# A mixture-of-experts kernel on one core: the routing's intermediate values in a PSUM bank of their own

## The chip, the core and the metric

The kernel runs on one core of one Trainium2 chip. Its engines are TensorE (PE in the profile; PEld is its loading of weights), VectorE (DVE), ScalarE (ACT), GpSimd (POOL) and the queue engine SyncE (SP). SBUF is the on-chip memory that all of them reach; PSUM is the small memory of eight banks into which TensorE writes, and which VectorE and ScalarE read and write too. The metric is the device time of one execution in microseconds (us), lower is better.

## The reference

Linear attention on 8 batches x 8 heads x 576 tokens x 64 channels, and then a layer of 8 experts on the 4608 rows of 512 channels, of which each row uses one. In outline (the maximum, the small constants and the scaling are left in, the reshapes left out):

```python
def phi(x):                       # x = q or k, scaled by 64 ** -0.25
    proj = einsum('bhsd,md->bhsm', x, omega)
    h = proj - sum(x * x, -1, keepdims=True) / 2.0
    h = h - max(h, -1, keepdims=True)
    return exp(h) / sqrt(m)
kv = einsum('bhsm,bhsd->bhmd', phi(k), v);  z = sum(phi(k), 2)
x = einsum('bhsm,bhmd->bhsd', phi(q), kv) / (einsum('bhsm,bhm->bhs', phi(q), z)[..., None] + 1e-06)

logits = x @ w_gate               # [4608, 8]
e_idx = argmax(logits, axis=1)
probs = softmax(logits)
gate_w = probs[arange(N), e_idx]
eom = 1.0 / (1.0 + exp(-(x @ w_output_gate)))
for e in range(8):
    mask = e_idx == e
    ye = maximum(x[mask] @ w1[e], 0.0) @ w2[e]      # 512 -> 1024 -> 512
    out[mask] = gate_w[mask, None] * eom[mask, e, None] * ye
```

## The kernel before

**Units, groups and items.** The tokens are treated in four groups of 1152 (two batches each, nine chunks of 128 rows). In each group the attention runs head by head: 32 units u (8 per group), each with projections `pp`, a minimum and a bias on VectorE (L525, L534, L538), exponentials on ScalarE (`ef`, L544), a high and a low half of most values (POOL makes the low halves: `xlo` L437, `es` L567, `vs` L588, `xs` L715), key-value sums `kv`, halves of them `kvs` on VectorE (L657, L659) and the result `pn`. When a group's attention is done, its rows are *routed*, and then items of up to 128 rows that belong to one expert go through that expert: 8, 8, 9 items after the first three groups and what is left after the fourth (38 in the profiled execution). An item n is a gather `gx` on POOL (L1344), a transposing DMA, a first projection in two halves `hA` and `hB` (L1381, 24 x 2 matmuls of which each half fills one bank `ph`), a rectifier on ScalarE and VectorE (L1388, L1392), a second projection `po` (L1404), a scaling `os` on ScalarE (L1456) that empties its bank, and a scatter on POOL (L1445). While a later group's attention runs, the items of the groups before it are woven in; after the fourth group only items are left.

**One routing.** It is a chain of some 55 small VectorE instructions of 1 to 250 columns with a few matmuls: `route` (L811 on: sum of the logits' halves, largest logit, which expert), `counts` on PE (how many rows of each expert stand ahead, into the bank `pos`), `ranks` and `places` (each row's place in its expert's list, and `place`, a 0/1 matrix of 128 x 1152), `gates`, two exponentials on ScalarE and `weigh` (the output's weight, saved to DRAM by a DMA as `scales`), then for the group's list `table`, `assign`, `lists`, `controls`, the matmuls `indices` into the bank `pid`, `listed` (the index list `gi` which the gathers use), and `advance`, which brings the state (`done`, `last`, `ahead`) up to date for the next group. All the values in between are small SBUF tiles named `r_...`, made by `small` and `per_slot` (L798, L801); most steps read two of them.

**What sets the order.** No engine's order is written by hand. `Plan.order` (L173) takes every step with its engines, an assumed cost, what it comes after, a rank and the PSUM banks that it takes and frees, and places steps one after the other: of those that could start first, the one with the least rank. The engines then run their instructions in that order, each in its own queue. Routing steps have the rank RANK_ROUTE + 80 j, far ahead of attention and items; `gates` and `weigh` stand 5 behind that, `advance` 40 behind (L1133, L1135, L1166). Of the eight banks, five ("a") serve attention and three ("b") the items; class "e" takes any, and is used by the first twelve units and by `pos` and `pid`.

## Time and profile before

| | us |
|---|---|
| median of 3 runs (699.2 to 703.88) | 701.48 |
| the profiled execution | 700.21 |
| its span, first to last instruction | 698.4 |
| PE busy | 613.5 (88%) |
| DVE busy | 444.4 (64%) |
| ACT busy | 406.1 (58%) |
| POOL busy | 326.6 (47%) |

The page names a line of the kernel, the engine, the operation and the tiles (out<-in). The view of stretches gives, for each, its length, then each engine's busy time with its count of instructions, the mean clock that TensorE was granted as a share of full speed, the share of the DMA engines and the bytes moved. In a timeline a row begins with its start and its length in us; a bracket at its end is the time that the engine stood idle just before, and what ended it. An answer on one line of the kernel gives the count and the minimum, median and maximum of its length in ns, and when it ran first and last. The mean granted clock of the whole execution is 0.948.

### The profile page before, as it was taken

The page shows a single profiled execution, that of the slowest core. Times are in us where ns is not written, and L with a number is a line of the kernel's source. Part 1 is how long each engine was busy: PE and PEld are TensorE (multiplying, and loading weights), DVE is VectorE, ACT ScalarE, POOL GpSimd, SP SyncE. Part 2 cuts the span into 40 slices and gives each one's busy share as a digit, 9 for nine tenths or more (in the row PEclk, how much of TensorE's full clock was granted, in tenths as well). Part 3 has the DMA queues.
Part 4 walks back from the last instruction along what each step waited for, and adds up shares of the span by engine and source line. Part 5 has one row for each costly group of instructions (what it writes and reads, how often), then busy time and mean ns, then how long its engine had stood idle before and what let it go on. Part 6 is the DMA issues. An engine that isn't in the chain of part 4 may idle for free. (4 is left out here: it accounts for less than half of the span.)

```text
span 698.4 us, 22925 instructions
## 1 busy us (share of the span) xinstructions
PE 613.5 (88%) x8763; PEld 471.3 (67%) x8763; DVE 444.4 (64%) x1260; ACT 406.1 (58%) x909; POOL 326.6 (47%) x207
## 2 busy tenths in 40 slices
PE   6999974888897987599979869999999899999982
PEld 6899863856674765577747637887777576776750
DVE  4997898966577789688648788663583521341160
ACT  5967795878686773797858538772341421431150
POOL 1333253568673875689827637964122121231210
PEclk9999996899998999799989989999999999999997
DMA  8656889999999996999999976769956634832630
GB/s 276 235 141 165 260 257 222 176 267 225 294 304 274 177 250 113 213 208 296 212 299 232 222 134 159 148 121 190 313 127 176 211 84 109 291 75 70 246 116 8
DMA packets 181033, 137.78 MB, mean 197 GB/s; under 512 B 139535, under 2 KB 162575, under 8 KB 179600
## 3 DMA queue, kind: packets, MB, share of 16 engines
q1 hardware_dynamic: 174800, 116.13, 68.2%
q0 software_dynamic: 6080, 19.72, 9.2%
q8 instruction: 83, 1.36, 0.8%
q14 instruction: 70, 0.57, 0.3%
HBM read 83.69 MB, written 19.69 MB: 148 GB/s over the span
## 5 line engine op out<-in xcount | busy, mean ns | idle before, releaser
L1381 PE MATMUL ph<-xt,w1h 128*128 128x128 f16 (+1 forms) x2432 | 205.0, 218 | 1.5 <-DMA xt<-gx 1.4
L544 ACT ACTIVATE ef<-pp,nb 128x128 f32<-128x128 f32 x576 | 164.2, 392 | 70.0 <-DVE nb L538 34.5
L1381 PE MATMUL ph<-xt,w1l 128*128 128x128 f16 (+1 forms) x1216 | 201.3, 218 | 0.4 <-DVEq L1305 0.4
L1381 PEld LDWEIGHTS <-w1h 128*128 128x128 f16 x2432 | 182.0, 99 | 8.7 <-DMA xt<-gx 1.6
L1392 DVE SCALAR_TENSOR_TENSOR hl<-ph,hh 128x512 f16<-128x512 f32 (+1 forms) x76 | 50.5, 666 | 128.9 <-ACTq L1310 77.9
L567 POOL TENSOR_TENSOR es<-ef,es 128x1152 f16<-128x1152 f32 x44 | 104.7, 2384 | 43.6 <-ACT es L565 22.6
L1404 PE MATMUL po<-w2h,hl 128*128 128x512 f16 x304 | 119.6, 393 | 5.4 <-DVE hl L1392 5.4
L1404 PE MATMUL po<-w2h,hh 128*128 128x512 f16 x304 | 120.1, 395 | 4.5 <-DVE w1l L369 2.4
L1404 PE MATMUL po<-w2l,hh 128*128 128x512 f16 x304 | 119.6, 393 | 0.0
L1381 PEld LDWEIGHTS <-w1l 128*128 128x128 f16 x1216 | 118.8, 99 | 0.6 <-DVEq L1305 0.6
L525 DVE TENSOR_REDUCE pp<-pp 128x3 f32<-128x384 f32 x192 | 102.7, 558 | 22.1 <-PE pp L503 21.7
L1344 POOL DMA_INDIRECT gx<-rows,gi x38 | 40.5, 1067 | 162.9 <-ACT os L1456 119.8
L1404 PEld LDWEIGHTS <-hh 128*128 128x128 f16 x608 | 57.3, 100 | 70.0 <-issue 9.9
L1388 ACT ACTIVATE hh<-ph 128x512 f16<-128x512 f32 (+1 forms) x76 | 44.7, 589 | 75.0 <-PE ph L1381 66.4
L1456 ACT ACTIVATE os<-po,gx 128x512 f32<-128x512 f32 x38 | 26.1, 687 | 92.5 <-PE po L1404 80.3
L715 POOL TENSOR_TENSOR xs<-xf,xs 128x576 f16<-128x576 f32 x32 | 41.1, 1285 | 64.5 <-DVE xs L711 27.5
L437 POOL TENSOR_TENSOR xlo<-xt,xhi 128x1152 f16<-128x1152 f32 x24 | 57.2, 2381 | 20.0 <-ACT xhi L430 20.0
L1404 PEld LDWEIGHTS <-hl 128*128 128x128 f16 x304 | 30.8, 101 | 45.0 <-DVE hl L1392 6.4
L503 PE MATMUL pp<-omh,xhi 64*128 64x128 f16 x432 | 45.3, 225 | 17.4 <-ACT ef L544 5.5
L565 ACT CAST es<-ef 128x1152 f16<-128x1152 f32 x44 | 51.6, 1176 | 10.7 <-DMA et<-es 8.0
L503 PEld LDWEIGHTS <-xhi 64*128 64x128 f16 x864 | 35.0, 98 | 29.1 <-issue 9.4
L681 PE MATMUL pn<-kvs,et 128*128 128x65 f16 (+1 forms) x960 | 41.2, 199 | 10.2 <-DVE kvs L659 4.1
(159 smaller groups left out, 1015.0 us busy)
## 6 DMA issues: line engine op xcount, KB each, us to landing
r<-w SPq DMA_DIRECT2D x10, 2048.0 KB, 9.4
xt<-kqt SPq DMA_DIRECT2D x32, 576.0 KB, 5.5
xn<-kqn SPq DMA_DIRECT2D x24, 576.0 KB, 7.3
rawv<-v SPq DMA_DIRECT2D x32, 325.0 KB, 5.3
rows<-xs SPq DMA_DIRECT2D x16, 576.0 KB, 5.8
r<-w SPq DMA_DIRECT2D x8, 512.0 KB, 10.3
ef<-w SPq DMA_DIRECT2D x2, 512.0 KB
et<-w SPq DMA_DIRECT2D x2, 512.0 KB, 7.6
```

The costliest lines, as they stand in the source:

```text
L437: lambda t0=t0, t1=t1: nc.gpsimd.tensor_tensor(out=xl(u)[:, t0:t1], in0=xt32(u)[:, t0:t1], in1=xh(u)[:, t0:t1], op=ALU.subtract),
L503: nc.tensor.matmul(banks["pp", 2 * u + i, g][:, c, :], x[r, t], w[r, :], start=(a == 0), stop=(a == len(ops) - 1))
L525: nc.vector.tensor_reduce(out=pp[:, 3, 0:3], in_=pp[:, 0:3, :], op=ALU.min, axis=AX.X)
L544: nc.scalar.activation(ef(n)[:, c, :], banks["pp", n, g][:, c % 3, :], AF.Exp, bias=nb(n)[:, c : c + 1], scale=-SK)
L565: nc.scalar.copy(es(slot_es(n))[:, 0], ef(n))
L567: nc.gpsimd.tensor_tensor(out=es(slot_es(n))[:, 1], in0=ef(n), in1=es(slot_es(n))[:, 0], op=ALU.subtract)
L681: nc.tensor.matmul(pn[lo:hi, c - c0, :], a[:, c, lo:hi], w[:, b, :], start=(i == 0), stop=(i == len(ops) - 1))
L715: nc.gpsimd.tensor_tensor(out=x[:, :, P + o : P + o + D], in0=xf(pr)[:, :, o : o + D], in1=x[:, :, o : o + D], op=ALU.subtract)
L1381: nc.tensor.matmul(ph[:, f4, 0:w_], w[qd][:, kk, fo : fo + P], xt(n)[:, x, 0:w_], start=(a == 0), stop=(a == 3 * KC - 1))
L1388: nc.scalar.activation(hh(n)[:, sl, 0:w_], banks["ph", n, g][:, :, 0:w_], AF.Relu)
L1392: nc.vector.scalar_tensor_tensor(out=hl(n)[:, sl, 0:w_], in0=banks["ph", n, g][:, :, 0:w_], scalar=0.0, in1=hh(n)[:, sl, 0:w_], op0=ALU.ma ...
L1404: nc.tensor.matmul(po, x(n)[:, f, :], w[f // 2][:, f % 2, :], start=(f == 0 and a == 0), stop=(f == FC - 1 and a == 2))
```

## The change

Each routing takes a PSUM bank of its own, `rt`, with its first step, and frees it with the last step of `advance` (`limits` in the fourth). The table `HOMES` gives most `r_...` values a range of columns in it, several of them the same range one after the other, and `inner` returns such a range. What ScalarE or a later step outside needs stays in SBUF (`top`, `rm`, `one`, `d`, `zs`, `tot`, `eq`, `itc`), and where a step would read two values of the bank, one of them is written a second time to SBUF (`avs`, `exs`, `turns`). The fourth group's long lists (24 slots) stay in SBUF.

Beside that: the constant half of `off` is written once at the start; `weigh` has one step less; the index list of the first three groups is made as an equality `eq` times a pair of constants (`cp`, copied to the bank from two more constant columns) instead of three steps; `gates` gets the rank R + 0.1, `advance` R + 3; `table` comes after `gates` too, and the step that frees the bank after all that still reads it. The core of the diff:

```diff
@@ constants
-C_END = C_CHUNK + NSC * NC
+C_BOTH = C_CHUNK + NSC * NC
+C_END = C_BOTH + 2 * NSC * NC
...
+    c[:, C_BOTH:C_END:2] = np.arange(P)[:, None]
+    c[:, C_BOTH + 1 : C_END : 2] = np.arange(NSC * NC) * P
@@ the bank
+    HOMES = {}
+    for names, width in (
+        ("l both", 2 * KM * NE), ("oh pk mine", NC * NE), ("z t8 cp", NC * NE), ("sm fin", KM), ("rank", NC), ("av_i", NE),
+        ("av", NE), ("start", NE), ("end", NE), ("ex", 2 * KM + 2), ("key", KM), ("ri here", KM), ("t1", NE), ("turn", NE),
+    ):
+        at = max((a + n for a, n in HOMES.values()), default=0)
+        HOMES.update({nm: (at, width) for nm in names.split()})
...
+    def inner(j, nm, sh, dt=F32):
+        a, n = HOMES[nm]
+        size = math.prod(sh)
+        assert size <= n
+        t = banks["rt", j][:, a : a + size]
...
+    def inner_slot(g, nm, lead, K, tail=()):
+        return per_slot(nm, lead, K, tail) if g == NG - 1 else inner(GROUPS[g], nm, [*lead, K, *tail])
@@ route, gates, weigh, ranks, places
-        l = small("l", [NC, 2 * NE])
+        l = inner(j, "l", [NC, 2 * NE])
...
-        z = small("z", [NC, NE])
+        z = inner(j, "z", [NC, NE])
...
-        nc.vector.tensor_scalar(zs, zs, 1.0, None, ALU.add)
-        yield
-        nc.vector.tensor_tensor(out=sm, in0=sm, in1=zs, op=ALU.mult)
+        nc.vector.scalar_tensor_tensor(out=sm, in0=zs, scalar=1.0, in1=sm, op0=ALU.add, op1=ALU.mult)
...
-        rank = small("rank", [NC])
+        rank = inner(j, "rank", [NC])
@@ table, assign
-        av = t["av"] = small("av", [NE])
+        av = inner(j, "av", [NE])
         nc.vector.tensor_tensor(out=av, in0=av_i, in1=done[:, 0, :], op=ALU.subtract)
         yield
+        t["av"] = small("avs", [NE])
+        nc.vector.tensor_tensor(out=t["av"], in0=av_i, in1=done[:, 0, :], op=ALU.subtract)
+        yield
...
-        off = t["off"] = small("off", [2, NE])
-        nc.vector.tensor_copy(off[:, 1, :], eidx)
-        yield
+        t["off"] = off
...
+        t["exs"] = small("exs", [max(KS) + 1])[:, 0 : K + 1]
+        nc.vector.tensor_copy(t["exs"], ex[:, 1, :])
+        yield
@@ lists (first three groups)
+            cp = inner(GROUPS[g], "cp", [nt, 2])
+            nc.vector.tensor_copy(cp, cft[:, C_BOTH : C_BOTH + 2 * nt].rearrange("p (c a) -> p c a", a=2))
+            yield
+            eq = small("eq", [(NSC - 1) * NC, max(EARLIER)], F16)[:, 0:nt, 0:K]
+            nc.vector.tensor_tensor(
+                out=eq,
+                in0=keys[:, 0:nt].unsqueeze(2).broadcast_to([P, nt, K]),
+                in1=t["key"].unsqueeze(1).broadcast_to([P, nt, K]),
+                op=ALU.is_equal,
+            )
+            yield
+            itc = t["itc"] = small("itc", [(NSC - 1) * NC, 2, max(EARLIER)], F16)[:, 0:nt, :, 0:K]
+            nc.vector.tensor_tensor(
+                out=itc,
+                in0=eq.unsqueeze(2).broadcast_to([P, nt, 2, K]),
+                in1=cp.unsqueeze(3).broadcast_to([P, nt, 2, K]),
+                op=ALU.mult,
+            )
+            return
@@ advance
-        turn = small("turn", [NE])
+        turn = inner(GROUPS[g], "turn", [NE])
         nc.vector.tensor_scalar(turn, eidx, last, float(NE), ALU.is_gt, ALU.mult)
         yield
+        turns = small("turns", [NE])
+        nc.vector.tensor_tensor(out=turns, in0=turn, in1=eidx, op=ALU.subtract)
+        yield
@@ the plan
+        chain(
+            "route", (0.37, 0.14, 0.14, 0.14, 0.14, 0.14), route, first, tiles=[("lga", j)],
+            bank=("e", ("rt", j), [512]),
+        )
...
-        chain("gates", (0.14, 0.14, 0.14), gates, [("route", j)], rank=R + 5)
+        chain("gates", (0.14, 0.14, 0.14), gates, [("route", j)], rank=R + 0.1)
...
-        chain("table", (0.07, 0.07, 0.08, 0.13, 0.08, 0.14, 0.08, 0.08, 0.08), table, [("ranks", j), *old])
+        chain("table", (0.07, 0.07, 0.08, 0.08, 0.13, 0.08, 0.14, 0.08, 0.08), table, [("ranks", j), ("gates", j), *old])
...
-                "advance", (0.07, 0.07, 0.08, 0.08, 0.08, 0.08, 0.08, 0.08, 0.08, 0.13), advance, [("controls", g)],
-                rank=R + 40,
+                "advance", (0.07, 0.07, 0.08, 0.08, 0.08, 0.08, 0.08, 0.08, 0.08, 0.08, 0.13), advance,
+                [("controls", g), ("lists", g), ("weigh", j), ("places", j)], rank=R + ADV, frees=[("rt", j)],
```

Where it stands in the instruction order is seen at three places. The first is VectorE in the second routing, where `weigh` and `table` run past each other, ahead of the `kvs` halves of the next unit. Before:

```order
L938 TENSOR_REDUCE r_tot_5424<-r_av_5318 128x1
L857 TENSOR_SCALAR r_sm_5309<-r_sm_5309 128x9
L941 TENSOR_REDUCE r_start_5429<-r_t8_5322 128x8
L859 TENSOR_SCALAR r_zs_5294<-r_zs_5294 128x9
L945 COPY r_off_5432<-cft_70 128x8
L861 TENSOR_TENSOR r_sm_5309<-r_sm_5309,r_zs_5294 128x9
L947 TENSOR_TENSOR r_off_5432<-done_84,r_start_5429 128x8
L863 RECIPROCAL scales_90<-r_sm_5309 128x9
L950 TENSOR_TENSOR r_end_5438<-r_start_5429,r_av_5318 128x8
L657 TENSOR_SCALAR kvs18_5441<-kv_18_5325 128x130
```

The same place after the change, where every value in `rt_1` lies in the bank of the second routing:

```order
L975 TENSOR_REDUCE r_tot_5282<-rt_1_5082 128x1
L1352 UNCONDITIONAL_BRANCH
L894 SCALAR_TENSOR_TENSOR rt_1_5082<-r_zs_5179,rt_1_5082 128x9
L978 TENSOR_REDUCE rt_1_5082<-rt_1_5082 128x8
L896 RECIPROCAL scales_91<-rt_1_5082 128x9
L982 TENSOR_TENSOR off_87<-done_84,rt_1_5082 128x8
L663 TENSOR_SCALAR kvs17_5340<-kv_17_5137 128x130
```

The scaling L857 (L892 now) has moved some rows up, L859 and L945 are gone, and of each pair of inputs one lies in the bank; the halves that follow are those of unit 17 instead of 18. The second place is VectorE at the end of the second routing, in `advance`, between the minima and biases of `pp`. Before:

```order
L1075 TENSOR_REDUCE last<-r_fin 128x1
L538 SCALAR_TENSOR_TENSOR nb_5749<-pp_0_5201,sqs_3982 128x3
L1078 TENSOR_SCALAR r_turn<-cft,last 128x8
L525 TENSOR_REDUCE pp_1_5232<-pp_1_5232 128x3
L1080 TENSOR_TENSOR r_turn<-r_turn,cft 128x8
```

And after:

```order
L1131 TENSOR_REDUCE last<-rt_5082 128x1
L663 TENSOR_SCALAR kvs_5685<-kv_5626 128x130
L1134 TENSOR_SCALAR rt_5082<-cft,last 128x8
L665 SCALAR_TENSOR_TENSOR kvs_5685<-kv_5626,kvs_5685 128x130
L1137 TENSOR_TENSOR r_turns<-rt_5082,cft 128x8
L531 TENSOR_REDUCE pp_2_5662<-pp_2_5662 128x3
L1139 TENSOR_TENSOR rt_5082<-rt_5082,cft 128x8
```

Here the steps of `advance` write to the bank (L1134) and to the SBUF copy `turns` (L1137), with `kvs` of a later unit between them. The third place is PE in the first routing, the head of the list matmuls `pid`. Before, unit 11's projections `pp_22` and `pp_23` have begun ahead of them:

```order
L503 MATMUL pp_22_1_2034<-omh_73,xlo11_1821 128x128
L503 LDWEIGHTS xlo11_1821
L503 MATMUL pp_23_1_2035<-omh_73,xlo11_1821 128x128
L1093 LDWEIGHTS place_89
L1190 TENSOR_LOAD ctl0_2062
L1093 MATMUL pid_0_2178<-r_itc_2059,place_89 128x16
```

After the change the last `pid` matmul is followed by the first matmul of unit 11:

```order
L1152 MATMUL pid_0_2008<-r_itc_2004,place_90 128x16
L509 LDWEIGHTS xhi11_1783
L1258 TENSOR_LOAD ctl0_1996
L509 MATMUL pp_22_0_2127<-omh_73,xhi11_1783 128x128
L509 LDWEIGHTS xhi11_1783
```

So two groups of unit 11's projections, which stood ahead of `pid`, now stand behind it.

More of the change, by code (lines that the diff above doesn't have):

```diff
@@ L1139, in routing @@
         )
+    ADV = 3
     def listing(g):
@@ L1151, in listing @@
         wide = 0.06 + 0.0085 * K
-        chain("table", (0.07, 0.07, 0.08, 0.13, 0.08, 0.14, 0.08, 0.08, 0.08), table, [("ranks", j), *old])
-        chain("assign", (wide, wide, 0.07, wide, 2 * wide, 2 * wide, 0.08), assign, [("table", g)])
+        chain("table", (0.07, 0.07, 0.08, 0.08, 0.13, 0.08, 0.14, 0.08, 0.08), table, [("ranks", j), ("gates", j), *old])
+        chain("assign", (wide, wide, 0.07, wide, 2 * wide, 2 * wide, 0.08, 0.08), assign, [("table", g)])
         each = 0.06 + 0.001 * nt * K
         own = [("ef", FREE)] if g == NG - 1 else []
-        chain("lists", (each, each, each), lists, [("assign", g), ("places", j)], tiles=own)
+        inside = j < NSC - 1
+        chain("lists", (0.1, each, 0.06 + 0.0021 * nt * K) if inside else (each, each, each), lists, [("assign", g), ("places", j)], tiles=own)
         chain("controls", (0.1, 0.08, 0.08, 0.08, 0.08), controls, [("assign", g)], rank=R + 1)
@@ L1164, in listing @@
             chain(
-                "advance", (0.07, 0.07, 0.08, 0.08, 0.08, 0.08, 0.08, 0.08, 0.08, 0.13), advance, [("controls", g)],
-                rank=R + 40,
-            )
-        else:
-            chain("limits", (0.08, wide, wide, 0.08, 0.08, 0.08, 0.08), limits, [("assign", g)], rank=R + 0.5)
+                "advance", (0.07, 0.07, 0.08, 0.08, 0.08, 0.08, 0.08, 0.08, 0.08, 0.08, 0.13), advance,
+                [("controls", g), ("lists", g), ("weigh", j), ("places", j)], rank=R + ADV, frees=[("rt", j)],
+            )
+        else:
+            chain(
+                "limits", (0.08, wide, wide, 0.08, 0.08, 0.08, 0.08), limits,
+                [("assign", g), ("controls", g), ("lists", g), ("weigh", j), ("places", j)], rank=R + 0.5, frees=[("rt", j)],
+            )
             plan.add(
```

55 lines of the change are left out of this document (32 added, 23 removed).

## Prediction

> **What bounds the kernel now.** I read the page's busy table first (PE, TensorE, busy for 88% of the span, so most of the time is fixed by matmuls), then the idle time of PE by stretch, and then, in the stretches where it idles, the rows of DVE (VectorE) and POOL (GpSimd) side by side. The table of stretches takes the four routings (first token group to fourth) alone:
>
> ```profile
> core 0: us, PE busy (x) PEld busy (x) DVE busy (x) ACT busy (x) POOL busy (x), PEclk, DMA share, GB/s
> 97.00:127.00 30.00, 17.73 (x253) 15.74 (x253) 27.53 (x110) 18.49 (x48) 14.35 (x9) 0.72 0.86 214
> 250.00:290.00 40.00, 26.86 (x403) 19.70 (x405) 35.72 (x117) 19.89 (x44) 23.54 (x16) 0.88 0.83 178
> 390.00:424.00 34.00, 26.95 (x395) 19.45 (x393) 31.28 (x101) 15.26 (x34) 17.93 (x12) 0.85 0.76 162
> 503.00:535.00 32.00, 31.58 (x394) 23.13 (x392) 21.98 (x69) 9.79 (x15) 6.41 (x6) 1.00 0.63 160
> ```
>
> In the first three DVE is busy for 27.5 of 30, 35.7 of 40 and 31.3 of 34 us, while PE stands for 12.3, 13.1 and 7.1 us and has a granted clock of 0.72 to 0.88. There DVE is the limit, not PE. The fourth is different: PE works 31.6 of 32 us, so nothing that speeds DVE up there can be worth more than 0.4 us.
>
> What DVE does in those stretches is the point. These are its long rows in the timeline, and then POOL's at the same times:
>
> ```profile
> 103.16 2.10 DVE L841 TENSOR_TENSOR r_z<-r_l,r_one 128x72 f32<-128x72 f32 x1
> ...
> 112.22 2.20 DVE L947 TENSOR_TENSOR r_off<-done,r_start 128x8 f32<-128x8 f32 x1
> ...
> 252.41 2.36 DVE L822 TENSOR_TENSOR r_oh<-r_l,r_top 128x72 f32<-128x72 f32 x1
> ...
> 261.82 4.46 DVE L857 TENSOR_SCALAR r_sm<-r_sm 128x9 f32<-128x9 f32 x1
> ...
> 275.58 4.27 DVE L1078 TENSOR_SCALAR r_turn<-cft,last 128x8 f32<-128x8 f32 x1
> ...
> 399.81 2.42 DVE L907 CAST keys<-r_ri 128x9 f32<-128x9 int32 x1
> ...
> 409.98 1.31 DVE L983 TENSOR_TENSOR r_key<-r_ex,cft 128x9 f32<-128x9 f32 x1
> 411.33 2.53 DVE L996 TENSOR_TENSOR r_itc<-keys,r_key 128x243 f16<-128x243 f32 x1
> ```
>
> ```profile
> 102.80 2.37 POOL L437 TENSOR_TENSOR xlo<-xt,xhi 128x1152 f16<-128x1152 f32 x1 [1.46 <-ACT xhi L430]
> ...
> 112.03 2.36 POOL L437 TENSOR_TENSOR xlo<-xt,xhi 128x1152 f16<-128x1152 f32 x1
> ...
> 249.96 4.71 POOL L567 TENSOR_TENSOR es<-ef,es 128x1152 f16<-128x1152 f32 x2
> ...
> 263.84 2.40 POOL L567 TENSOR_TENSOR es<-ef,es 128x1152 f16<-128x1152 f32 x1
> ...
> 277.45 2.37 POOL L437 TENSOR_TENSOR xlo<-xt,xhi 128x1152 f16<-128x1152 f32 x1
> ...
> 399.78 2.41 POOL L567 TENSOR_TENSOR es<-ef,es 128x1152 f16<-128x1152 f32 x1
> ...
> 411.22 2.36 POOL L437 TENSOR_TENSOR xlo<-xt,xhi 128x1152 f16<-128x1152 f32 x1
> ```
>
> An operation on 8 or 9 columns that lasts 4.46 us ends at 266.28, and POOL's elementwise work ends at 266.24; L841 ends at 105.26, POOL at 105.17; L1078 at 279.85, POOL at 279.82. Each of these long rows has all its tensors in SBUF and ends within 0.3 us of the end of POOL's work. Unhindered, the same lines are short, and lines with a PSUM operand are never long (answers by line: count, then minimum/median/maximum in ns):
>
> ```profile
> L947 DVE TENSOR_TENSOR r_off<-done,r_start x4: 156/163/2199, 112.2 to 519.0; 128x8 f32<-128x8 f32 x4
> L857 DVE TENSOR_SCALAR r_sm<-r_sm x4: 168/175/4464, 107.0 to 518.6; 128x9 f32<-128x9 f32 x4
> L1078 DVE TENSOR_SCALAR r_turn<-cft,last x3: 222/223/4268, 124.5 to 419.5; 128x8 f32<-128x8 f32 x3
> L824 DVE TENSOR_TENSOR r_oh<-r_oh,cft x4: 218/230/235, 101.8 to 506.5; 128x72 f32<-128x72 f32 x4
> L887 DVE TENSOR_TENSOR r_pk<-pos,cnt x4: 216/222/234, 106.6 to 514.7; 128x72 f32<-128x72 f32 x4
> L534 DVE SCALAR_TENSOR_TENSOR pp<-pp,sqs x144: 152/160/170, 86.2 to 469.3; 128x3 f32<-128x3 f32 x144
> ```
>
> L534 reads one operand from PSUM and one from SBUF. It ran 144 times between 86 and 469 us, in which POOL is busy about half the time, and its worst is 170 ns.
>
> **The change part by part.** First, the operands. Nearly every routing step gets at least one PSUM operand, as L534 and L887 have, so the wait for POOL goes. What that is worth is not DVE's time but PE's, at the places where PE stood for it:
>
> ```profile
> 115.52 0.28 PE L503 MATMUL pp<-omh,xhi 64*128 64x128 f16 x1 [2.91 <-DVE r_ex L968]
> ...
> 256.06 0.19 PE L871 MATMUL pos<-r_one,cmt 128*128 128x72 f16 x1 [1.54 <-DVE r_one L832]
> ...
> 267.55 0.84 PE L681 MATMUL pn<-kvs,et 128*128 128x65 f16 x12 [4.08 <-DVE kvs L659]
> ...
> 281.69 0.21 PE L503 MATMUL pp<-omh,xhi 64*128 64x128 f16 x1 [2.14 <-ACT ef L544]
> ...
> 404.78 1.10 PE L637 MATMUL kv<-vs,es 128*128 128x65 f16 x30 [1.61 <-DVE xf L694]
> ...
> 414.72 0.87 PE L1093 MATMUL pid<-r_itc,place 128*128 128x18 f16 x27 [3.93 <-DVE ctl L1024]
> ```
>
> - First routing: L947 loses 2.20 - 0.16 = 2.0 us inside PE's gap of 2.91. Credit 2.0. L841 loses 1.9, but no gap above lies at 103 to 105: credit 0.
> - Second: L822 loses 2.36 - 0.23 (L824 has its shape) = 2.1 ahead of the counting matmuls, whose gap is 1.54: credit 1.5. L857 loses 4.46 - 0.17 = 4.3 with the `kvs` steps queued behind it, for which PE waits 4.08: credit 4.1. L1078 loses 4.27 - 0.22 = 4.05; behind it stand a reduction and bias of `pp`, behind them ScalarE's exponentials (ACT), behind them PE for 2.14: credit 2.1.
> - Third: L907 loses 2.42 - 0.17 = 2.2 against a gap of 1.61: credit 1.6. L983 and L996 lose 1.31 - 0.16 and, with 0.4 as an estimate for its free length from L824's 0.23 and 171 more columns, 2.53 - 0.4; together 3.3 in the list chain that `pid` waits 3.93 for: credit 3.3.
>
> Sum 2.0 + 7.7 + 4.9 = 14.6 us. Second, the clock. After those gaps the granted clock is half:
>
> ```profile
> 267.00:270.00 3.00, 2.45 (x29) 2.45 (x30) 3.00 (x16) 0.89 (x3) 0.00 (x0) 0.50 0.62 93
> 284.00:294.00 10.00, 6.26 (x97) 5.61 (x98) 7.51 (x28) 7.97 (x19) 8.62 (x6) 0.50 1.01 233
> 414.00:420.00 6.00, 5.28 (x38) 2.33 (x38) 4.07 (x27) 2.70 (x7) 0.98 (x1) 0.50 0.58 178
> ```
>
> Busy time at half clock is half lost: 1.2, 3.1 and 2.6 us. The first and third follow gaps that vanish almost whole; of the second I take half, 1.6. Credit 5.4.
>
> Third, the length of an operation with PSUM operands. L887 (PSUM and SBUF) takes 222 ns, L824 (SBUF alone) 230, same shape: cost 0. Some 56 instructions per routing touch the bank, so an error of 10 ns would be 0.6 us in each. The Trainium skill speaks against this: "Perfetto Trace Analysis", section "Optimizing Scalar/DVE Operations", gives VectorE an overhead of about 60 ns on SBUF and 125 on PSUM; the two rows do not show it. By that figure the estimate is 3 x 56 x 65 ns, 10.9 us of DVE more in the three tight routings, and a forecast near 694.
>
> Fourth, steps added and dropped: copies of `av`, `ex` and `turn` come in, the copy L945 and one step of `weigh` go, and the list product is one wide step for two: about three instructions more over the kernel, 0.5 us at 0.16 each, hidden beyond that. A copy from SBUF into PSUM (`cp`, `turn`) is a form without a row: 0 by L824, 2 us a time if it still waits as L947 did. I take 0, since it has one SBUF operand as L534. The Trainium skill ("SBUF — State Buffer", "Who interferes with whom") says likewise that one SBUF input outside the 2-port modes does not contend; no row here has this form.
>
> Fifth, the bank: one of eight is held from the first reduction to the end of `advance` (99 to 125 us, 251 to 281, 389 to 423 in the rows of before). The planner may give it one of the three banks of the expert steps; then the second half of an item's first projection waits till the item before it has left its output bank. That can be late:
>
> ```profile
> 277.95 0.38 PE L1404 MATMUL po<-w2h,hl 128*128 128x512 f16 x1
> ...
> 280.75 1.82 ACT L544 ACTIVATE ef<-pp,nb 128x128 f32<-128x128 f32 x6 [3.72 <-DVE nb L538]
> 283.45 0.69 ACT L1456 ACTIVATE os<-po,gx 128x512 f32<-128x512 f32 x1 [0.88 <-ACTq L1305]
> ```
>
> The output was complete at 278.33 and the bank free at 284.14, 5.8 us later: ACT had stood 3.72 us for a bias that was queued behind L1078. Between the two stands half of the next item's first projection, 48 matmuls of L1381, of which the second routing ran two:
>
> ```profile
> 251.00:281.00 30.00, 6.64 (x96) 6.37 (x96) 0.94 0.81 167
> ```
>
> That is 3.3 us of cover each. So 0 to 5.8 an item, with two items in each of the second and third routing; I take 2.5, one late item less its cover.
>
> Sixth, the order. `gates` and `advance` get an earlier rank, and `table` waits for `gates`. In the first routing `pid` now stands ahead of all of unit 11 on PE: the gathers come earlier, but PE has less to do till the lists are there. Either way a microsecond or two; no row decides, 0. On POOL three gathers move ahead of unit 8's low half (L715), which runs on into a stretch where POOL stood idle for `gi`. `advance` now stands behind `weigh` and so behind ACT's two gate exponentials, which `scales` waited for already.
>
> Sum: 700.2 (the profiled execution: span 698.4 and 1.8 around it) - 14.6 - 5.4 + 2.5 = 682.7. The median of the runs is 701.5, 1.3 above, so the forecast is **684.0 us**.
>
> **The rivals.** *The gain is eaten by the next wait.* Where the stall and PE's gap agree almost exactly (L822 and L857: 1.5 + 4.1, and the 1.2 of clock) it must come, but the other gaps have other waits beside them: ACT, the transposes, the expert switch. Then 700.2 - 6.8 + 2.5 + 1.3 = 697.2. For it: 2.91 of PE's 12.3 idle us in the first routing is all I could tie to a stall. Against it: DVE's shares of 89 to 92%.
>
> *The bank costs more than the ports give, and it is slower.* Four items at 5.8 = 23.2, the clock credit gone since PE stands again: 700.2 - 14.6 + 23.2 + 1.3 = 710.1. It decides above 14.6 / 4 = 3.7 us an item. Against it: with L1078 short, the late row loses its cause.
>
> *The change does not do what it says*: POOL blocks a DVE step with one PSUM operand as well, or a later all-SBUF step takes the wait over. 700 to 702. L534's 170 ns speaks against the first.
>
> *PSUM operands are dearer.* A quarter more than L887's 222 ns, 55 ns, on each of 3 x 56 steps is 9.2 us of DVE in the tight routings, of which its busy share of 0.9 reaches PE: 684.0 + 8.3 = 692.3. The equal rows L887 and L824 speak against it. The Trainium skill's rule on PSUM overhead, cited above, is of this kind.
>
> **How the numbers follow.** Forecast 0.56; gain eaten 0.18; bank 0.12; does not do it 0.08; PSUM dearer 0.06. Some 1% (7 us) is what measurement can tell from no change, so faster is below 694.5, slower above 708.5. Faster: 0.56 + 0.06, and a third of the eaten case, 0.06, 0.68 in all. Slower 0.12. Within 1%: 0.20. Low end: all the DVE time of the eight rows, 1.9 + 2.0 + 2.1 + 4.3 + 4.05 + 2.2 + 3.3 = 19.9, and the clock 6.9, no cost: 700.2 - 26.8 + 1.3 = 674.7; shorter stalls that I did not list may add, so 672. High end 702, which takes in the eaten case and leaves the bank's.
>
> **What would show it.** Right: the routing's lines all under 0.6 us beside POOL's work, the fan-out (L814 to L1082) some 5 to 10 us shorter in the second and third routing, PE's gaps of 4.08 and 3.93 gone, granted clock over 0.9 there. Wrong: DVE rows of 2 us in steps with a PSUM operand, lines with the bank at 290 ns instead of 225, or new PE gaps ahead of `hB`, released by `os`.

## The result, and the profile after

The changed kernel takes 678.81 us in the median of 4 runs (673.83 to 680.11), where the kernel before took 700.67 beside it: a ratio of 0.967, 95% interval 0.961 to 0.973. In a later comparison on another chip it took 676.79 against 694.96, 0.972 (0.967 to 0.978). It is faster, and the forecast was 684.

The profiled execution took 680.11 us, its span 678.3, its mean granted clock 0.960 (before: 700.21, 698.4 and 0.948). This is the table of stretches for the first three routings of the changed kernel, with the same lengths as in the table of before (the routings lie at other times now):

```profile
97.00:127.00 30.00, 18.61 (x250) 17.11 (x249) 23.81 (x110) 19.43 (x52) 13.94 (x9) 0.73 0.92 232
239.00:279.00 40.00, 32.40 (x510) 24.36 (x508) 29.64 (x128) 24.83 (x61) 27.47 (x18) 0.87 0.88 201
381.00:415.00 34.00, 30.08 (x503) 22.59 (x500) 26.27 (x115) 19.11 (x43) 21.73 (x14) 1.00 0.83 185
```

VectorE (DVE, the third pair of numbers after the length) is busy for 23.8, 29.6 and 26.3 us in them, where it was 27.5, 35.7 and 31.3, and does at least as many instructions in each. TensorE (PE) works 5.5 us more in the second and 3.1 us more in the third. These stretches do not begin at the same step of the routing in both kernels. Cut from the first reduction of each routing (30, 34 and 34 us long), VectorE's busy time is 27.7, 30.7 and 31.3 us before and 25.6, 25.6 and 25.5 us after. GpSimd (POOL) is busier than before in all three of these (15.3, 18.5 and 17.7 us before, 16.4, 21.5 and 21.5 after), so the waits did not go because there was less to wait for.

The answers by line (count, minimum/median/maximum in ns) for the steps that were long before, now with `rt`, the bank, among their operands. L876 was L841, L892 was L857, L1134 was L1078 and L982 was L947:

```profile
L876 DVE TENSOR_TENSOR rt<-rt,r_one x4: 229/230/241, 105.3 to 497.4; 128x72 f32<-128x72 f32 x4
...
L892 DVE TENSOR_SCALAR rt<-rt x4: 175/176/176, 110.8 to 499.4; 128x9 f32<-128x9 f32 x4
...
L1134 DVE TENSOR_SCALAR rt<-cft,last x3: 218/222/222, 123.3 to 406.6; 128x8 f32<-128x8 f32 x3
...
L982 DVE TENSOR_TENSOR off<-done,rt x4: 101/132/164, 111.6 to 505.2; 128x8 f32<-128x8 f32 x4
...
L1033 DVE COPY rt<-cft x3: 180/186/207, 116.1 to 397.0; 128x18 f32<-128x18 f32 x1, 128x36 f32<-128x36 f32 x1, 128x54 f32<-128x54 f32 x1
```

The worst of L892 is 176 ns where L857 had 4464, and of L1134 222 where L1078 had 4268. L1033 is the copy from SBUF into PSUM, the form for which the trace of before had no row.

Where the time came from is seen when both spans are cut at the start of each routing. First the kernel before, then the changed one; the second number of a row is PE's busy time:

```profile
0.00:99.10 99.10, 87.66 (x1235) 80.37 (x1235) 81.17 (x241) 75.13 (x216) 33.29 (x23) 1.00 0.71 219
99.10:251.30 152.20, 125.07 (x1939) 96.61 (x1938) 114.56 (x342) 113.18 (x259) 95.68 (x55) 0.90 1.02 242
251.30:389.50 138.20, 117.86 (x1852) 88.60 (x1851) 103.68 (x312) 98.28 (x215) 95.06 (x56) 0.93 0.98 230
389.50:503.90 114.40, 106.74 (x1680) 81.58 (x1677) 77.45 (x241) 61.46 (x138) 66.58 (x42) 0.96 0.80 179
503.90:698.40 194.50, 176.15 (x2071) 124.17 (x2068) 67.54 (x131) 58.03 (x82) 36.00 (x33) 0.97 0.49 139
```

```profile
0.00:101.40 101.40, 90.27 (x1235) 83.12 (x1236) 80.24 (x242) 74.82 (x216) 32.32 (x23) 0.95 0.71 220
101.40:240.50 139.10, 117.79 (x1880) 92.85 (x1879) 106.11 (x337) 107.31 (x247) 94.01 (x54) 0.94 1.08 254
240.50:382.30 141.80, 128.37 (x2074) 97.48 (x2071) 104.79 (x333) 108.08 (x240) 102.31 (x61) 0.94 1.02 241
382.30:493.60 111.30, 104.79 (x1607) 78.86 (x1602) 68.64 (x230) 62.23 (x133) 62.13 (x40) 1.00 0.78 184
493.60:678.30 184.70, 167.12 (x1982) 117.97 (x1979) 63.45 (x125) 52.20 (x75) 34.19 (x32) 0.97 0.47 138
```

The lengths alone mislead, since the planner moved matmuls from one part to another (1852 became 2074 in the third row). Length less PE's busy time does not depend on that: PE stood for 11.4, 27.1, 20.3, 7.7 and 18.4 us before, 84.9 in sum, and stands for 11.1, 21.3, 13.4, 6.5 and 17.6 now, 70.0 in sum. That is 15.0 us. The same 8763 matmuls are busy for 608.3 us instead of 613.5, 5.1 us less, at a mean granted clock of 0.960 for 0.948. Together 20.1 us of span.

### The profile page after: what moved, and what is told of

It reads as the page before. It is cut to its first block, busy times and chain, and to the rows that moved or that the text cites. A ratio compares the mean times of both kernels' runs of the same rounds, so it can differ in the third digit from the quotient of the medians.

```text
span 678.3 us, 22888 instructions
## 1 busy us (share of the span) xinstructions
PE 608.3 (90%) x8763; PEld 470.3 (69%) x8763; DVE 423.2 (62%) x1264; ACT 404.6 (60%) x909; POOL 325.0 (48%) x207
## 5 line engine op out<-in xcount | busy, mean ns | idle before, releaser
L1472 PE MATMUL po<-w2h,hh 128*128 128x512 f16 x304 | 116.4, 383 | 2.4 <-DVE hl L1466 2.1
L1472 PE MATMUL po<-w2h,hl 128*128 128x512 f16 x304 | 116.0, 382 | 1.5 <-DVE hl L1460 1.5
L1472 PE MATMUL po<-w2l,hh 128*128 128x512 f16 x304 | 116.1, 382 | 0.2 <-issue 0.2
L687 PE MATMUL pn<-kvs,et 128*128 128x65 f16 (+1 forms) x960 | 42.6, 202 | 15.7 <-DMA et<-es 6.4
```

What stands on the lines that cost most here:

```text
L687: nc.tensor.matmul(pn[lo:hi, c - c0, :], a[:, c, lo:hi], w[:, b, :], start=(i == 0), stop=(i == len(ops) - 1))
L1472: nc.tensor.matmul(po, x(n)[:, f, :], w[f // 2][:, f % 2, :], start=(f == 0 and a == 0), stop=(f == FC - 1 and a == 2))
```

## The experiments

The changed kernel differs from the one before in two things that the comparison above cannot part: where the operands lie, and the order of the instructions, which the planner sets anew when steps, dependences and a bank change. Two theories follow. **The port**: VectorE's steps waited for GpSimd, and the bank ends that. **The order**: the gain comes from the new order or the new steps. Below, each ratio is to the kernel before, run beside that kernel on its own chip; the kernel before had a median of 695.0 to 695.8 us in all three groups of runs.

### The values back in SBUF, the order kept

```diff
             for _, name, shape in s["bank"]:
                 b = plan.bank_of[name]
+                if name[0] == "rt":
+                    banks[name] = sb.tile([P, 392], F32, tag="rtsb", name=..., bufs=1)
+                    continue
                 banks[name] = ps.tile([P, *shape], F32, tag=f"bank{b}", name=...)
```

> The changed kernel with one thing put back: the routing's values between its steps lie in a tile of SBUF (392 floats a partition, one tile that the four routings use in turn) in place of the PSUM bank. The planner still gives the bank to them for the same stretch, so the bank is as scarce as in the changed kernel, and VectorE and TensorE keep the changed kernel's order of instructions. Theory of the shared port (VectorE's steps whose tensors all lie in SBUF wait until GpSimd's elementwise operations are over): waits of 1 to 4.5 us come back to the routing's steps, 15 to 30 us of them in sum, a routing takes 26 to 33 us again from its first step to the fan-out matrix where the changed kernel takes 23 to 26, and the time goes back to 694 to 704 us. Theory of the order (the time came from the other order, the cheaper list step and the shorter weighing, and the port only happens to be there): 676 to 683 us, as the changed kernel.

Measured: 689.15 us, ratio 0.989 (0.985 to 0.994). The changed kernel's is 0.972 (0.967 to 0.978), and the intervals do not touch. By the medians, 12.4 us come back from the operands alone. The time lies between what the two theories expected (694 to 704, and 676 to 683), nearer to the port's side: neither has the whole. The traces of the two kernels have the same instructions in the same order on every engine, so the difference is that of the operands' place and of what follows from it. With SBUF, seventeen routing steps are 0.4 to 4.3 us longer than with the bank, 29.7 us in sum, and the first three routings take 27.3, 33.0 and 32.2 us from the first step to the fan-out matrix `ahead`, against 23.1, 22.0 and 25.4 in the changed kernel's later execution. That is what the port theory expected of the kernel with SBUF. The waits are on other lines than in the kernel before. Answers by line of this kernel:

```profile
L998 DVE TENSOR_TENSOR rt<-rt,cft x3: 222/1134/4552, 109.2 to 404.1; 128x64 f32<-128x64 f32 x2, 128x72 f32<-128x72 f32 x1
...
L1033 DVE COPY rt<-cft x3: 166/171/2198, 114.9 to 407.5; 128x18 f32<-128x18 f32 x1, 128x36 f32<-128x36 f32 x1, 128x54 f32<-128x54 f32 x1
```

And this is how one of them reaches TensorE. Timeline of this kernel at the start of its third routing:

```profile
390.83 2.36 POOL L443 TENSOR_TENSOR xlo<-xt,xhi 128x1152 f16<-128x1152 f32 x1
...
391.35 1.93 DVE L859 TENSOR_TENSOR rt<-rt,cft 128x72 f32<-128x72 f32 x1
393.15 2.36 POOL L573 TENSOR_TENSOR es<-ef,es 128x1152 f16<-128x1152 f32 x1
...
393.60 2.01 DVE L867 TENSOR_TENSOR r_one<-rt,r_rm 128x72 f16<-128x72 f32 x1
...
395.66 0.21 PE L904 MATMUL pos<-r_one,cmt 128*128 128x72 f16 x1 [3.67 <-DVE r_one L867]
```

L859 ends at 393.28, 0.09 us after GpSimd's first subtraction (393.19); L867 begins when the second one runs already and ends at 395.61, 0.10 us after that. TensorE stands 3.67 us for the counts. The same place in the changed kernel, in its later profiled execution:

```profile
379.65 0.22 DVE L867 TENSOR_TENSOR r_one<-rt,r_rm 128x72 f16<-128x72 f32 x1
379.68 2.38 POOL L443 TENSOR_TENSOR xlo<-xt,xhi 128x1152 f16<-128x1152 f32 x1
379.86 0.22 DVE L873 TENSOR_TENSOR r_d<-rt,r_top 128x72 f32<-128x72 f32 x1
...
380.68 0.20 PE L904 MATMUL pos<-r_one,cmt 128*128 128x72 f16 x1
```

L873 begins inside a subtraction and takes 0.22 us. Over the whole span VectorE does the same 1264 instructions in both kernels, and takes 24.0 us more with the values in SBUF. The page's row of the run with SBUF, then of the changed kernel:

```profile
PE 612.4 (89%) x8763; PEld 473.2 (69%) x8763; DVE 446.6 (65%) x1264; ACT 405.1 (59%) x909; POOL 326.5 (47%) x207
```

```profile
PE 609.3 (90%) x8763; PEld 471.5 (70%) x8763; DVE 422.6 (63%) x1264; ACT 406.1 (60%) x909; POOL 326.2 (48%) x207
```

Of these 24 us the spans show 687.8 - 674.9 = 12.9: 3.1 of TensorE's busy time, and 9.8 of standing.

The bank is not free either, and this pair shows it. Three steps of the third routing with the bank, from the changed kernel's first execution, then the same with SBUF, where no step is stalled up to the start of L944:

```profile
389.17 0.17 DVE L936 CAST rt<-rt 128x9 int32<-128x9 f32 x1
389.38 0.17 DVE L961 TENSOR_SCALAR rt<-cnt 128x8 int32<-128x8 f32 x1
...
390.70 1.34 DVE L944 TENSOR_TENSOR place<-cmt,rt 128x1152 f16<-128x1152 f16 x1
```

```profile
398.46 0.16 DVE L936 CAST rt<-rt 128x9 int32<-128x9 f32 x1
398.53 0.16 DVE L961 TENSOR_SCALAR rt<-cnt 128x8 int32<-128x8 f32 x1
...
399.27 3.50 DVE L944 TENSOR_TENSOR place<-cmt,rt 128x1152 f16<-128x1152 f16 x1
```

The steps are equally long, but with the bank L961 starts only when L936 has ended, 0.21 us after it, and with SBUF 0.07 us after it, though it does not read what L936 writes. From L936 to L944 it is 1.53 us against 0.81. The trace has a semaphore wait at L961 with the bank and none with SBUF; over the four routings 187 of 228 VectorE steps have one, against 145. In 102 pairs of neighbouring routing steps without a stall in either kernel, the second starts 209 ns after the first with the bank and 125 ns with SBUF, in the median; over all these pairs the bank adds 7.2 us. So the differences of the pairs are what is left after this cost. Why the program waits there was not looked into, and what fewer such waits would give was not tried.

### The same pair in another order

One number of the planner that has nothing to do with the routing was moved, in the changed kernel and in the run with the values in SBUF:

```diff
-TIE = 0.1
+TIE = 0.12
```

> The changed kernel with one number of the planner moved that has nothing to do with the routing: steps count as tied within 0.12 us in place of 0.10, which sets another order nearly everywhere. If what the change brings is in the operands, the routing's steps stay without a wait and the time stays 2 to 4 percent below the kernel before give or take the order's chance: 672 to 688 us. If the changed kernel's order is a lucky one, this is at 688 to 700 us, and the difference to the changed kernel is the size of that luck.

> The kernel with the planner's tie at 0.12 us (684.1 us, 1.6 percent below the kernel before) with the routing's values in the SBUF tile in place of the bank, the planner's bank kept: the same pair as the first, in a second order. Theory of the shared port: waits of 1 to 4.5 us are back on the routing's steps, 20 to 30 us in sum, and the time is 8 to 16 us above that kernel, 692 to 700 us. Theory that the first pair's 12 us were an accident of one order: within 4 us of it, 680 to 688 us.

| | values in PSUM | values in SBUF | difference |
|---|---|---|---|
| the planner's order, tie at 0.10 | 676.79, ratio 0.972 (0.967 to 0.978) | 689.15, 0.989 (0.985 to 0.994) | 12.4 us |
| tie at 0.12 | 684.08, 0.984 (0.979 to 0.988) | 703.06, 1.013 (1.005 to 1.021) | 19.0 us |

The run with the bank stays 1.6 percent below the kernel before, as the port theory had it (672 to 688). The operands are worth 12 us in one order and 19 in the other, where I had expected 8 to 16; the second run with SBUF lies above the 692 to 700 us that I had given it. The two columns were run on different chips. By their ratios to the kernel before the differences are 11.8 and 20.2 us, with some 5 and 6 us to either side as an estimate from the intervals. That the operands are worth something is shown in both orders; that they are worth more in the second is hardly shown. The two rows also show the order by itself: the same steps and operands are 7.3 us slower in another order with the bank and 13.9 us slower without it.

### The bank, and the plan without the operands

The next kernel has the values in SBUF and no bank at all:

```diff
-        t = banks["rt", j][:, a : a + size]
+        t = held(j)[:, a : a + size]          # one SBUF tile
...
-            bank=("e", ("rt", j), [512]),
```

> As the run with the values in SBUF, but the planner is not told of a bank either: no bank is taken by the routing, and the items' matmuls have all of class e as in the kernel before, with the changed kernel's steps and dependences. The instructions' order moves where the planner now finds a bank free. If holding the bank costs what I put down for it (2.5 us, at most 5.8 for each item kept waiting), this kernel is 1 to 6 us faster than the run with the values in SBUF and the bank taken; if the bank costs nothing, the two agree to 2 us. By the theory of the shared port it stays above 690 us and shows waits of 1 to 4.5 us on the routing's steps; by the theory of the order it is at 674 to 683 us.

Measured: 699.85 us, ratio 1.006 (1.001 to 1.011). It was expected 1 to 6 us faster than the run that holds the bank and is 10.7 us slower. Its ten runs lie between 691.91 and 706.14. A bank that costs would show the other sign, but the order moved with it, so the run does not say whether the taken bank costs anything. It stays above 690 us and has routing steps of up to 3.1 us, as the port theory had it.

Then the kernel before with a part of the planner's side of the change: the bank, what `advance` comes after and its rank. (The earlier rank of `gates`, `table` after `gates`, and the new steps are not in it.)

```diff
+        chain("route", ..., tiles=[("lga", j)], bank=("e", ("rt", j), [512]))
...
-                [("controls", g)], rank=R + 40,
+                [("controls", g), ("lists", g), ("weigh", j), ("places", j)], rank=R + 3, frees=[("rt", j)],
```

> The kernel before, with its steps and its values in SBUF, and only what the change tells the planner: each routing is given one of the banks of class e from its first step to the end of its advance chain (nothing is put into the bank), and the advance chain comes after the lists, the controls, the weighing and the places. It separates the order from the operands. The run with the values in SBUF and the bank taken was 10 us faster than the one with neither, so the taken bank itself changed the order for the better, against the 2.5 us that I had put down as its cost. Theory that the taken bank is worth that in general: 685 to 690 us. Theory that an order of the planner is worth plus or minus 1 percent by chance whatever moves it: anything from 688 to 705 us, most likely at the kernel before, 695 to 700.

Measured: 692.95 us, ratio 0.998 (0.992 to 1.003). The bank taken in the plan and these dependences neither cost nor give what can be measured. So the 10.7 us between the two SBUF kernels are not a general worth of a taken bank. Four kernels with the values in SBUF now stand at 0.989, 0.998, 1.006 and 1.013 of the kernel before: about 1.2 percent to each side by order (and steps), with the operands the same.

### The wait by itself

> Measures the disputed cost by itself and computes nothing of the reference (its output is zeros): GpSimd runs 60 subtractions of 128x1152 float32 and then 20 memsets, all in SBUF; beside it VectorE goes 40 times through thirteen steps of 128x72 float32, which differ only in where their operands lie, with no semaphore between the two engines. Theory of the shared port: two tensors from SBUF into SBUF, scalar steps, copies and scalar-tensor steps from SBUF into SBUF take 1 us and more while GpSimd subtracts, and 0.1 to 0.3 us beside memsets and afterwards; those with one operand or the result in PSUM take 0.1 to 0.3 us throughout. Two tensors from SBUF into PSUM: waits too, if it is the reading that counts, and runs free, if any PSUM operand is enough. Rival, that VectorE is slowed by GpSimd's traffic in general: all the forms are longer by a like factor beside the subtractions.

The tiles a, b and o lie in SBUF; `bank` is PSUM. Answers by line over the whole run, of whose 285 us GpSimd is busy for the first 240 (60 subtractions of 2.61 us, with the 20 memsets of 3.93 us among the first of them):

```profile
L282 DVE TENSOR_TENSOR o<-a,b x40: 167/922/2635, 1.2 to 255.7; 128x72 f32<-128x72 f32 x40
...
L283 DVE TENSOR_TENSOR o<-bank,b x40: 210/217/222, 1.3 to 270.3; 128x72 f32<-128x72 f32 x40
...
L286 DVE TENSOR_SCALAR o<-a x40: 180/2591/32117, 1.4 to 256.0; 128x72 f32<-128x72 f32 x40
...
L293 DVE TENSOR_REDUCE o<-a x40: 164/212/221, 2.2 to 256.3; 128x9 f32<-128x72 f32 x40
```

There is no semaphore between the two engines, so nothing in the program makes one wait for the other. The forms with PSUM on one side never pass 242 ns (one of them is shown), and neither does the reduction, though all of it lies in SBUF. It is not a general slowing by GpSimd's traffic either. I counted the steps that began while a GpSimd operation had more than 0.5 us to go. Two tensors from SBUF (L282) waited in 20 of 20 cases beside a subtraction, which reads SBUF, and in none of 10 beside a memset, which only writes. The scalar step (L286) waited in all 30, beside either. The Trainium skill ("SBUF — State Buffer", "Who interferes with whom") says this of two SBUF inputs: they contend with a GpSimd instruction that reads SBUF, not with one that only writes. The counts agree. What the two engines share, a port or something else, no run here shows by itself; below, "the port" stands for this pattern of waits.

One form had not been caught beside a subtraction, two SBUF tensors into PSUM:

> Measures one more form by itself and computes nothing of the reference (its output is zeros): GpSimd runs 60 subtractions of 128x1152 float32 in SBUF, and VectorE in a fixed order two tensors from SBUF into PSUM (lines 286 and 288), a copy from SBUF to SBUF (290), from SBUF into PSUM (292) and from PSUM to SBUF (294), each followed by two scalar steps that read PSUM. The run of the thirteen forms left the first of these open: its step of two SBUF tensors into PSUM never began with more than 0.5 us of a subtraction before it. If reading two tensors from SBUF is what waits, lines 286 and 288 take up to 2.6 us beside a subtraction; if any operand in PSUM is enough, as the change's name has it the other way round, they take 0.2 us. The copies with PSUM on one side take 0.2 us by both, and line 290 waits.

```profile
L288 DVE TENSOR_TENSOR bank<-a,b x40: 241/1176/2120, 2.0 to 229.7; 128x72 f32<-128x72 f32 x40
...
L290 DVE COPY o<-a x40: 186/1188/2193, 2.7 to 230.4; 128x72 f32<-128x72 f32 x40
...
L292 DVE COPY bank<-a x40: 235/236/236, 3.3 to 231.0; 128x72 f32<-128x72 f32 x40
```

Two tensors read from SBUF wait even when the result goes to PSUM, up to 2.12 us; one tensor read from SBUF into PSUM does not. So for a step of two tensors it is the reading that counts. In the changed kernel the second copies of `av`, `ex` and `turn` give each later pair one operand from either place; a pair with both operands in the bank was not tried.

### One more step out of the way

Of the steps left on VectorE, the cast of the attention's high half (L717, SBUF to SBUF) still waits. It was given to ScalarE, first with the planner told, then in VectorE's place in the order, and that also with the tie at 0.12:

```diff
-            nc.vector.tensor_copy(halves(xs(pr).bitcast(F16)...), halves(xf(pr)...))
+            nc.scalar.copy(halves(xs(pr).bitcast(F16)...), halves(xf(pr)...))
...
-            ("xh", u), ("DVE",), 0.37, hi_half, ...
+            ("xh", u), ("ACT",), 0.62, hi_half, ...     # only in the first of the three
```

> The changed kernel with one more step taken out of GpSimd's way: the high half of the attention's output (128x576, float32 to float16, SBUF to SBUF, 32 times) is made by ScalarE instead of VectorE. In the changed kernel eleven of these steps on VectorE are over 0.15 us too long, 10.6 us in sum, all beside GpSimd's elementwise work. Theory of the shared port: those waits vanish, VectorE is busy 20 to 25 us less and ScalarE some 20 us more; as VectorE bounds only the routings, 2 to 6 us come out of it, 672 to 677 us. Rival, the wait was off the path by now: 677 to 681 us. Rival, ScalarE's exponentials and weight casts now come late in its place: over 682 us.

> The high half on ScalarE again, but now the planner still takes it for a VectorE step of 0.37 us, so that every other instruction keeps its place and only this one changes its engine. Theory of the shared port: the waits of 10.6 us on this step are gone with nothing else moved, and the time is 1 to 5 us below the changed kernel of these rounds. Rival, the waits were off the path: within 1 us of it. Rival, ScalarE's longer step in the chain from the attention to the transposes keeps TensorE: 2 to 6 us above it.

> The kernel with the planner's tie at 0.12 us with the high half cast by ScalarE in VectorE's place in the order: the second pair for that edit. If the 4 us by which it was faster in the first order come from the waits on this step (13.6 us of them in this order, 10 us in the first), it is 3 to 8 us below that kernel, 676 to 681 us. If they were scatter, 682 to 687 us.

Measured: 685.51 us, ratio 0.989 (0.981 to 0.998), with the planner told; 672.65 us, 0.968 (0.962 to 0.975), in place; 684.14 us, 0.985 (0.978 to 0.992), in place with the tie at 0.12. L717 in the changed kernel and in the second of these:

```profile
L717 DVE CAST xs<-xf x32: 449/459/2577, 24.8 to 468.4; 128x576 f16<-128x576 f32 x32
```

```profile
L717 ACT CAST xs<-xf x32: 661/672/965, 25.3 to 470.3; 128x576 f16<-128x576 f32 x32
```

The waits up to 2.58 us are gone, and VectorE is busy for 402.2 us instead of 422.6. But the time is 4.1 us lower in one order, with intervals that overlap, and 0.1 us higher in the other. No gain is shown, which fits waits that lie off the path by now; the path itself was not followed. With the planner told, the time is 8.7 us higher than the changed kernel's. The same edit in place does not do that, so it is put down to the new order. The 672.65 us are the lowest median of all, and not distinguishable from the changed kernel's 676.79.

### The changed kernel once more

> The changed kernel once more, on the chip and in the rounds of the three that follow, since the runs with the values in SBUF shared rounds with the kernel before only (their kernel before at 695.1 us where it had been 700.7). Theory of the shared port: 672 to 681 us, 2.5 to 3.5 percent below the kernel before, so that the values in SBUF (689 us in the same order) cost 8 to 15 us. Rival, most of the gain was the spread between sessions: 684 to 690 us.

Measured: 676.79 us, ratio 0.972 (0.967 to 0.978). It is the changed kernel's value in all the differences above. It was run beside the tie at 0.12, the plan without the operands and the first cast in place; the runs with the values in SBUF were made on other chips, each beside the kernel before.

## Why the prediction was right, and where it was not

The forecast of 684.0 is 5 us above the measured 678.81 and inside its range, and the side was right. Its mechanism, the port, was confirmed by the forms and by both pairs. By its own steps:

**The operands and PE's gaps (14.6 us), and the clock (5.4).** Against the kernel before, PE stands 15.0 us less and is busy for 5.1 us less. The near agreement is partly luck: the comparison holds the order too. The pair in one order gives 9.8 and 3.1 us to the operands, the pair at the other tie 77.9 against 84.6 us of standing, 6.7, and 606.5 against 614.3 us of busy time, 7.8. So the term was 20.0 for what measured 12.4 and 19.0. I credited each whole gap whose releaser had been stalled, and in the changed kernel gaps of like size stand at new places (PE's rows in its timeline):

```profile
113.71 1.13 PE L687 MATMUL pn<-kvs,et 128*128 128x65 f16 x18 [4.27 <-DVE kvs L665]
...
269.06 0.26 PE L509 MATMUL pp<-omh,xhi 64*128 64x128 f16 x1 [3.12 <-ACTq L1373]
```

The 4.08 us for `kvs` in the second routing and the 3.93 for the third's lists are gone, as said. But in the first routing PE now waits 4.27 us for a `kvs` that stands among the unhindered routing steps, and the second stops 3.12 us at the expert switch and 2.45 us for ScalarE's exponentials. My rival "eaten by the next wait" said just that of these other waits. It did not take most of the gain: its 697.2 is far off. How much it took is not shown, since these gaps change from one execution to the next (in the later one of the same kernel they are 2.63, 0.97 and 1.10 us, with one of 2.81 us elsewhere), and with the values in SBUF, in the same order, the first is there too, at 3.40 us, so it is not what a vanished stall left behind.

**The clock's places.** I said over 0.9 in the second and third routing, and that the half-clock stretches after the first and third of the quoted gaps would go. The third is at 1.00 (0.85 before), which is right. The second is at 0.87 where it was 0.88 in the same 40 us, which is wrong for that stretch: a half-clock stretch follows the 3.12 us gap now. That gap stands behind the routing; from its first reduction to the fan-out matrix the second routing has 1.00, where it had 0.94. The first was at 0.72 and is at 0.73.

**The length with PSUM operands (0).** Right for the length, and the length was the wrong thing to price. L876 has 230 ns where L824 had 230 in SBUF, and L892 176 where L857's median was 175. But with the bank the steps start further apart, as shown above: 7.2 us of VectorE's time in the four routings, which the sum had at nothing. The rival "PSUM operands are dearer" (55 ns on each step, 9.2 us of VectorE) had about the right size, by another way than longer steps; its 692.3 us did not come. What this cost takes from the time was not measured by itself. In the forms measured alone, after GpSimd had ended, the size can be told; means of groups by line:

```profile
L282 DVE TENSOR_TENSOR o<-a,b 128x72 f32<-128x72 f32 x7 | 1.5, 216 | 0.0
...
L283 DVE TENSOR_TENSOR o<-bank,b 128x72 f32<-128x72 f32 x10 | 2.2, 220 | 0.0
...
L286 DVE TENSOR_SCALAR o<-a 128x72 f32<-128x72 f32 x8 | 1.5, 187 | 0.0
...
L287 DVE TENSOR_SCALAR bank<-a 128x72 f32<-128x72 f32 x10 | 2.3, 228 | 0.1
```

Two-tensor steps cost 4 ns more with one operand in PSUM, scalar steps of 72 columns 41 ns more; at the routing's 9 columns (L892) it was 1 ns. The Trainium skill ("VectorE: DVE Perf Modes", "Mode 2×_2P — use both read ports for one tensor") has a one-source step between two SBUF tensors read through both ports at double rate, which would make such a difference grow with the columns, as the rows show. The Trainium skill's figures ("Perfetto Trace Analysis", "Optimizing Scalar/DVE Operations"), some 65 ns more on PSUM, are not borne out by either form. The starts do not show them either: where nothing waits, the next step begins 132 ns after L282 and 139 after L283, 103 after L286 and about 135 after L287.

**Added and dropped steps (0).** Right as far as seen: the copy into PSUM (L1033) takes 180 to 207 ns and does not wait. In the run with SBUF the same copy lost 2.0 us.

**The bank (2.5 us lost).** Not seen. The kernel before with the bank taken in its plan is at 0.998 (0.992 to 1.003), and the changed kernel's three tight routings show no gap of over 1 us ahead of an item's second half. The rival by which the bank made it slower, 710.1, falls with it.

**The order (0, "no row decides").** This is the step that was mis-sized. The run with the values in SBUF and the changed kernel's order is still 5.9 us faster than the kernel before (695.06 to 689.15), where I had nothing for the order and 2.5 us of loss for the bank. So 20.0 - 2.5 = 17.5 us forecast stand against 12.4 + 5.9 = 18.3 measured: in this order a term that was too large and one that was missing nearly made each other up, and that the forecast came so close is luck. The order's part is no merit of the change; another tie turns it into a loss. What part of it belongs to the new steps and dependences was not separated.

**What would show it.** The fan-out (first reduction to `ahead`) was to be 5 to 10 us shorter in the second and third routing. For the third, before and after:

```profile
389.45 0.46 DVE L814 TENSOR_REDUCE r_l<-lga 128x144 f32<-128x288 f32 x1
...
422.48 0.21 DVE L1082 TENSOR_TENSOR ahead<-r_turn 128x64 f32<-128x64 f32 x1
```

```profile
382.31 0.46 DVE L849 TENSOR_REDUCE rt<-lga 128x144 f32<-128x288 f32 x1
...
407.69 0.22 DVE L1141 TENSOR_TENSOR ahead<-rt,r_turns 128x64 f32<-128x64 f32 x1
```

33.2 us became 25.6, 7.6 less; the second's 29.3 became 23.3, 6.0 less. "All under 0.6 us" was said too widely: the wide `place` step takes its own 1.34 us, the list step of the third routing 0.66 and the fourth routing's lists 1.05. No routing step waits for GpSimd: these three are as long in the run with SBUF where they are not stalled.

## What to carry to other kernels

When short VectorE steps take 1 to 5 us now and then, compare their ends with the ends of GpSimd's elementwise work. If they agree within 0.1 us, put one of two tensors into PSUM, or the input or the result of a scalar step or copy; moving only the result of a two-tensor step does not help. Then compare the starts of the steps too, and not only their lengths: here neighbours in the bank start 0.21 us apart instead of 0.125. Credit a gap of TensorE with less than the stall that ends it, since another wait can be near: of 24 us that VectorE gained here, 13 reached the end in one order. And where a planner sets the order anew, measure the edit in the same order, and in a second one, before a percent is called its gain.

## What the runs showed that I had not expected

A VectorE step that waits for GpSimd does not get its turn when the operation ahead ends, if GpSimd has the next one ready. In the run of the forms, one scalar step and the copy behind it:

```profile
99.60 3.93 POOL L299 MEMSET w<- 128x4608 f32 x1
99.80 32.12 DVE L286 TENSOR_SCALAR o<-a 128x72 f32<-128x72 f32 x1
99.90 32.05 DVE L289 COPY o<-a 128x72 f32<-128x72 f32 x1
...
129.26 5.29 POOL L297 TENSOR_TENSOR z<-x,y 128x1152 f32<-128x1152 f32 x2
```

The step waited 32 us, through ten GpSimd operations, and came in between the two subtractions of the last row (131.87 to 131.94). Most others of its kind waited for one. The 4.46 us of L857 in the kernel before look like a small case of the same: it began while GpSimd issued a scatter and ended with the second of the two subtractions behind that (1.47 and 2.40 us). What decides who gets the turn was not found out.
